# A group-norm kernel on one core: another engine leads the exit of the critical section, and most semaphores are cleared inside it

## The chip, the core and the metric

The kernel runs on one core of a Trainium2 chip. The core has five engines with their own instruction streams: PE (TensorE, matrix multiply), DVE (VectorE), ACT (ScalarE), POOL (GpSimd) and SP (SyncE), which here only issues DMA transfers and waits. The engines meet through numbered semaphores: an instruction can wait until a semaphore has reached a value, and can raise one when it is done. A DMA transfer raises its semaphore by 16 when it has landed.

The metric is the device time of the program in microseconds. Three runs of the kernel before gave 633.89, 633.71 and 632.71 us, median 633.71 us.

## The reference

The input x is bf16 of shape 128 x 1024 x 32 x 16 (134 MB), and so is the output. The 1024 channels fall into 32 groups of 32 channels; a group of one sample has 32 * 512 = 16384 numbers, which are brought to mean 0 and variance 1 and then scaled and shifted per channel:

```
xr = x.reshape(B, G, C // G, H, W)
mu = xr.mean(axis=(2, 3, 4), keepdims=True)
var = ((xr - mu) ** 2).mean(axis=(2, 3, 4), keepdims=True)
xn = (xr - mu) / jnp.sqrt(var + 1e-5)
xn = xn.reshape(B, C, H, W)
return xn * g[None, :, None, None] + b[None, :, None, None]
```

## The kernel before

One partition of the on-chip memory holds one group of one sample, so that a tile of 128 partitions holds 4 samples: 128 x 16384 bf16, 4 MB. There are 32 tiles and six slots for them (`xs`); a tile is loaded into its slot, normalised in place and stored from there, and the slot's next load waits until that store has landed.

Per tile, PE sums the partition's 16384 numbers with 32 matmuls against the identity into one PSUM tile (`sums`, L186 and L202). ACT takes a rough mean from the first channel (L210), then squares and sums the shifted numbers in four parts (L221), and takes the root of the variance (L230). DVE makes mean, variance, scale and bias from these (L237 to L277, instructions on a few numbers per partition) and applies them in 32 passes of 512 columns (L287). PE, ACT and DVE each run their part in a loop over rounds of six tiles; their waits name a semaphore per slot.

SP's stream is written out by hand, without a loop: L141 to L149. It issues six loads, and then alternately the store of a tile (L135, waits for DVE's last pass) and the load of a later one (L130, waits for an older store). All transfers go through SP's one queue. At the end, L150 and L151 let SP wait until the last store of each slot has landed. POOL only builds the identity at the start (L157, L167).

All of it stands in one critical section (L58), in which the framework orders nothing and adds no semaphore. What it adds lies around the section, and the change is about that. The instructions added carry the line L58 (entry and exit of the section) and L348 (the line of the launch that opens and closes the tile context; L337 is where the program object is made). They are:

- **Entry.** One engine, the section's leader, raises a semaphore, and all five wait for it in a branch. The leader is SP.
- **Exit.** The leader raises a second semaphore when it leaves the section (L58, semaphore 208 in the trace). Each of the five engines waits for it in a Drain (an instruction that lets the engine finish what it has begun) and then raises a semaphore of its own. The leader waits for those five in two event-semaphore instructions and a NOP.
- **End of the context** (L348). SP has one more Drain, which by the program waits for all engines; the waits are left out where SP has already made them. Then comes a barrier: every engine drains and raises the semaphore 96, POOL waits until the other four have, and lets them go by semaphore 97. POOL drains again and clears, in one instruction (EVENT_SEMAPHORE_RANGE_CLEAR), all semaphores that the context has given out, 99 to 212, which are 114. A second barrier of the same form ends the program.

Each semaphore of the kernel is made by a helper of two lines (L63), from the context, which is why the context clears them at its end:

```
def sem(name):
    return tc.alloc_semaphore(name)
```

Of the kernel before, what the change touches and what calls it, by code (L numbers as in the profile page):

```python
# [16 lines left out]
SLOTS = 6  # L17
# [5 lines left out]
def kernel(  # L23
# [13 lines left out]
    nc = tc.nc  # L37
# [17 lines left out]
    g_v = g.rearrange("(q k) -> q k", q=G)  # L55
    b_v = b.rearrange("(q k) -> q k", q=G)

    ctx.enter_context(tc.tile_critical())  # L58

    def sb(name, shape, dtype):  # L60
        return ctx.enter_context(nc.sbuf_tensor(name, shape, dtype))

    def sem(name):  # L63
        return tc.alloc_semaphore(name)

    xs = [sb(f"x{j}", [P, F], BF16) for j in range(SLOTS)]
    ps = [
# [32 lines left out]
    def sems(name):  # L100
        return [sem(f"{name}{j}") for j in range(SLOTS)]

    s_load = sems("load")
    s_store = sems("store")
    s_sum = sems("sum")
    s_shift = sems("shift")
    s_part = [sems(f"part{k}_") for k in range(SQ_PARTS)]
# [7 lines left out]
    s_bia = sems("bia")  # L115
    s_done = sems("done")
    s_gb = sem("gb")
    s_gbf = sem("gbf")
    s_eps = sem("eps")
    s_ones = sem("ones")  # L120
    s_half = sem("half")
    s_eye = sem("eye")

    sp, pe, act, dve, pool = nc.sync, nc.tensor, nc.scalar, nc.vector, nc.gpsimd

    def load(i):
        j, n = (i + FIRST) % SLOTS, i // SLOTS
        if n > 0:
            sp.wait_ge(s_store[j], 16 * n)
        sp.dma_start(out=xs[j][:], in_=x_v[i]).then_inc(s_load[j], 16)  # L130

    def store(i):
        j, n = (i + FIRST) % SLOTS, i // SLOTS
        sp.wait_ge(s_done[j], n + 1)
        sp.dma_start(out=o_v[i], in_=xs[j][:]).then_inc(s_store[j], 16)  # L135
# [10 lines left out]
    for i in range(NT):  # L146
        store(i)
        if i >= 1 and i + SLOTS - 1 < NT:
            load(i + SLOTS - 1)  # L149
    for j in range(SLOTS):  # L150
        sp.wait_ge(s_store[j], 16 * len(range((j - FIRST) % SLOTS, NT, SLOTS)))  # L151

# [169 lines left out]
            normalise(j, n)  # L322


# [1 line left out]
_INS = ['x', 'g', 'b']  # L326
_OUTS = [((128, 1024, 32, 16), 'bfloat16')]
# [25 lines left out]
```

## Time and profile before

| | |
|---|---|
| median of 3 runs | 633.71 us (632.71 to 633.89) |
| the profiled execution's own time | 633.21 us |
| its span, first to last instruction | 631.5 us |
| time outside the span (633.21 - 631.5) | 1.7 us |
| DMA, read and written | 268 MB, 425 GB/s over the span |
| ACT, DVE, PE busy | 519.3, 394.8, 284.3 us |
| last store issued on SP | 608.9 us |
| last store seen landed by SP (last L151) | 628.9 us |

The span is what lies between the first and the last instruction that carries a line of the program. Engine names with a q (SPq, POOLq) are the instructions that an engine's sequencer handles itself: waits, branches, drains, NOPs, clears, and DMA issues. In the view of one line's instructions, a row gives the engine, the operation and its count, the shortest, middle and longest duration in ns, and the start of the first and the last in us.

### The profile page before, as it was taken

Reading aid. Unit: us, or ns where it says so; the run is one execution under the profiler, and the core shown is the slowest. Engines: PE = TensorE matmul, PEld = TensorE weight load, DVE = VectorE, ACT = ScalarE, POOL = GpSimd, SP = SyncE. Lnnn points to the kernel's source line nnn. Section 1 sums busy time; section 2 is a strip of 40 time slices with the busy share of each in tenths; the row PEclk is TensorE's granted clock in tenths of the full one; section 3 lists DMA queues with packets and bytes.
Section 4 is the critical chain, followed back from the end, with each engine's and each line's share of the span. In section 5 each row is a group of like instructions: output and inputs, shape, how many; then the busy total and the mean of one; then the engine's idle time right before and its main releaser. Section 6 shows DMA issues by size and latency. Waiting matters only on the chain.

```text
span 631.5 us, 2991 instructions
## 1 busy us (share of the span) xinstructions
PE 284.3 (45%) x1024; PEld 3.3 (1%) x32; DVE 394.8 (63%) x1316; ACT 519.3 (82%) x354; POOL 0.8 (0%) x6
## 2 busy tenths in 40 slices
PE   1968405553445633456433654334553346543300
PEld 0000000000000000000000000000000000000000
DVE  0177777666666677777655676555775557765550
ACT  2999999999999999998788978889888888888800
POOL 0000000000000000000000000000000000000000
PEclk9999958765787667876678776778766787767755
DMA  8999999999999999999999999999999999999995
GB/s 363 430 430 413 440 438 432 431 430 430 432 432 428 432 430 432 432 432 432 430 432 438 434 432 432 436 440 436 430 432 434 432 432 432 434 432 432 432 432 233
DMA packets 9485, 268.51 MB, mean 425 GB/s; under 512 B 1288, under 2 KB 1288, under 8 KB 1288
## 3 DMA queue, kind: packets, MB, share of 16 engines
q1 hardware_dynamic: 9480, 268.46, 98.9%
q14 instruction: 4, 0.03, 0.0%
q8 instruction: 1, 0.02, 0.0%
HBM read 134.23 MB, written 134.22 MB: 425 GB/s over the span
## 4 chain that ended last, share of the span: by engine, by line
DMA 73%; ACT 18%; DVE 4%; issue 1%; SPq 1%; DVEq 0%; ACTq 0%
DMA out_dram<-x 66%; ACT js L221 17%; DMA x<-in_x_dram 7%; DVE x L287 3%; ACT ja L210 1%; SPq L130 1%; ACT std L230 0%; DVE jv L261 0%; DVE nd L252 0%; DVE d L248 0%; DVE bia L277 0%; DVE scl L273 0%; DVE rstd L271 0%; DVEq L247 0%; ACTq L307 0%
## 5 line engine op out<-in xcount | busy, mean ns | idle before, releaser
L221 ACT ACTIVATE js<-x,nshift 128x4096 bf16<-128x4096 bf16 x128 | 474.7, 3708 | 4.1
L287 DVE TENSOR_SCALAR x<-x,scl,bia 128x512 bf16<-128x512 bf16 x1024 | 333.6, 405 | 1.2
L186 PE MATMUL ps<-x,eye 128*128 128x512 bf16 x992 | 272.4, 443 | 0.0
L202 PE MATMUL ps<-x,eye 128*128 128x512 bf16 x32 | 18.4, 574 | 305.7 <-DMA x<-in_x_dram 305.7
L248 DVE TENSOR_TENSOR d<-negmean,nshift 128x1 f32<-128x1 f32 x32 | 5.1, 159 | 169.2 <-ACT js L221 169.2
L210 ACT ACTIVATE ja<-x 128x512 bf16<-128x512 bf16 x32 | 19.9, 623 | 47.5 <-DMA x<-in_x_dram 46.9
L230 ACT ACTIVATE std<-var,eps_t 128x1 f32<-128x1 f32 x32 | 9.4, 294 | 25.8 <-DVE jv L261 25.8
L237 DVE TENSOR_SCALAR_CACHE_REDUCE jd<-ps 128x512 bf16<-128x512 f32 x32 | 21.9, 685 | 13.4 <-PE ps L186 13.1
L221 ACT ACTIVATION_READ_ACCUMULATOR js<-x,nshift 128x1 f32 x128 | 23.9, 186 | 0.0
L271 DVE RECIPROCAL rstd<-std 128x1 f32<-128x1 f32 x32 | 5.2, 163 | 11.6 <-ACT std L230 11.6
L277 DVE SCALAR_TENSOR_TENSOR bia<-scl,negmean,bet 128x32 f32<-128x32 f32 x32 | 8.0, 251 | 1.1
L273 DVE TENSOR_SCALAR scl<-gam,rstd 128x32 f32<-128x32 f32 x32 | 7.7, 242 | 1.1
L179 DVE CAST gam<-gam_b 128x32 f32<-128x32 bf16 x1 | 0.2, 180 | 13.1 <-DMA bet_b<-in_b_dram 13.1
L261 DVE TENSOR_SCALAR_CACHE_REDUCE jv<-sq,nd 128x4 f32<-128x4 f32 x32 | 6.9, 217 | 1.1
L252 DVE TENSOR_SCALAR nd<-d 128x1 f32<-128x1 f32 x32 | 6.8, 214 | 1.1
L202 PEld LDWEIGHTS ps<-x,eye 128*128 128x128 bf16 x32 | 3.3, 103 | 577.3 <-DMA x<-in_x_dram 577.3
L210 ACT ACTIVATION_READ_ACCUMULATOR ja<-x 128x1 f32 x32 | 6.0, 186 | 0.0
L261 DVE DVE_READ_ACCUMULATOR jv<-sq,nd 128x1 f32 x32 | 2.6, 82 | 0.0
L237 DVE DVE_READ_ACCUMULATOR jd<-ps 128x1 f32 x32 | 2.6, 81 | 0.0
L177 ACT ACT_TABLE_LOAD x1 | 1.3, 1283 | 1.0 <-SPq L58 1.0
L154 DVE MEMSET eps_t<- 128x1 f32 x1 | 0.1, 59 | 1.1 <-SPq L58 1.1
L157 POOL TENSOR_SCALAR_AFFINE_SELECT half<-ones 128x128 bf16<-128x128 bf16 x1 | 0.3, 292 | 0.9 <-DVE ones L155 0.9
(8 smaller groups left out, 1.2 us busy)
## 6 DMA issues: line engine op xcount, KB each, us to landing
x<-in_x_dram SPq DMA_DIRECT2D x32, 4096.0 KB, 29.1
out_dram<-x SPq DMA_DIRECT2D x32, 4096.0 KB, 38.3
gam_b<-in_g_dram SPq DMA_DIRECT2D x1, 8.0 KB
bet_b<-in_b_dram SPq DMA_DIRECT2D x1, 8.0 KB
```

What stands on the lines that cost most here:

```text
L130: sp.dma_start(out=xs[j][:], in_=x_v[i]).then_inc(s_load[j], 16)
L186: return pe.add_instruction(mybir.InstMatmult(name=nc.get_next_instruction_name(), ins=[pe.lower_ap(rhs), first.ins[1]], outs=[first.outs[0]],
L202: m = pe.matmul(out=ps[j][:], lhsT=eye[:], rhs=xs[j][:, 0:MM_FREE], start=True, stop=False)
L210: act.activation(out=ja[:], in_=xs[j][:, 0:HW], func=ACT.Identity, scale=-1.0 / HW, accum_out=nshift[j][:],).then_inc(s_shift[j], 1)
L221: act.activation(out=js[:], in_=xs[j][:, k * SQ : (k + 1) * SQ], func=ACT.Square, bias=nshift[j][:], scale=1.0, accum_out=sq[j][:, k : k + 1],
L230: act.activation(out=std[j][:], in_=var[j][:], func=ACT.Sqrt, bias=eps_t[:], scale=1.0).then_inc(s_std[j], 1)
L237: dve.tensor_scalar(out=jd[:], in0=ps[j][:], scalar1=-inv_n, scalar2=None, op0=ALU.mult, op1=ALU.add, accum_out=negmean[j][:],).then_inc(s ...
L252: dve.tensor_scalar(out=nd2[j][:], in0=d[j][:], scalar1=d[j][:], scalar2=-1.0, op0=ALU.mult, op1=ALU.mult,).then_inc(s_nd2[j], 1)
L261: dve.tensor_scalar(out=jv[:], in0=sq[j][:], scalar1=inv_n, scalar2=nd2[j][:], op0=ALU.mult, op1=ALU.add, accum_out=var[j][:],).then_inc(s ...
L273: dve.tensor_scalar(out=scl[j][:], in0=gam[:], scalar1=rstd[j][:], scalar2=None, op0=ALU.mult).then_inc(s_scl[j], 1)
L277: dve.scalar_tensor_tensor(out=bia[j][:], in0=scl[j][:], scalar=negmean[j][:], in1=bet[:], op0=ALU.mult, op1=ALU.add,).then_inc(s_bia[j], 1)
L287: v = dve.tensor_scalar(out=xs[j][:, k * HW : (k + 1) * HW], in0=xs[j][:, k * HW : (k + 1) * HW], scalar1=scl[j][:, k : k + 1], scalar2=bi ...
```

## The change

The critical section gets two arguments: ACT is its leader (`sync_engine`), and POOL is not drained at its exit (`no_gpsimd_drain`). The kernel's semaphores, except the six of the stores and a new one named `gone`, are taken from the program object and not from the context, so that the context doesn't clear them. SP raises `gone` after it has issued the last store, and before its final waits. POOL waits for `gone` as the last thing in the section, and clears the kernel's own semaphores there as one range: 99 to 200, 102 of them. For the context's clear at the end, 13 are left: 201 to 213, which are the six of the stores, `gone`, and the six that the framework uses at entry and exit.

```
-    ctx.enter_context(tc.tile_critical())
+    ctx.enter_context(tc.tile_critical(
+            sync_engine=mybir.EngineType.Activation, no_gpsimd_drain=True
+        ))
...
+    all_sems = []
+
     def sem(name):
-        return tc.alloc_semaphore(name)
+        all_sems.append(nc.alloc_semaphore(name))
+        return all_sems[-1]
...
-    s_store = sems("store")
...
+    s_store = [tc.alloc_semaphore(f"store{j}") for j in range(SLOTS)]
+    s_gone = tc.alloc_semaphore("gone")
...
         if i >= 1 and i + SLOTS - 1 < NT:
             load(i + SLOTS - 1)
+    sp.sem_inc(s_gone, 1)
     for j in range(SLOTS):
         sp.wait_ge(s_store[j], 16 * len(range((j - FIRST) % SLOTS, NT, SLOTS)))
...
             normalise(j, n)
+    pool.wait_ge(s_gone, 1)
+    pool.sem_clear(range(all_sems[0].num, all_sems[-1].num + 1))
```

In the built program, this moves the following. At entry, ACT has the NOP that raises the semaphore, and SP no longer. At exit, ACT raises the leader's semaphore as soon as its own loop is done; the Drains of PE, DVE, SP and ACT and a NOP on POOL wait for it; ACT makes the three waits for the five engines. SP has no event-semaphore of the leader and no NOP; after the branch that ends its final waits comes its exit Drain, then two event-semaphore instructions and the Drain at the end of the context, which now carry the waits for the other engines, and then the barrier. The barriers, the second Drain of POOL and the order of clear and second barrier stay. The work inside the section is the same on every engine, instruction by instruction.

## The prediction

> **What bounds the kernel now.** I read the chain of waits first, then the waits on SP's own queue, then the DMA view, and last the rows of the added lines. The chain, by engine and line:
>
> ```profile
> DMA 73%; ACT 18%; DVE 4%; issue 1%; SPq 1%; DVEq 0%; ACTq 0%
> DMA out_dram<-x 66%; ACT js L221 17%; DMA x<-in_x_dram 7%; DVE x L287 3%; ACT ja L210 1%; SPq L130 1%; ACT std L230 0%; DVE jv L261 0%; DVE nd L252 0%; DVE d L248 0%; DVE bia L277 0%; DVE scl L273 0%; DVE rstd L271 0%; DVEq L247 0%; ACTq L307 0%
> ```
>
> The kernel is bound by its transfers: 268 MB through one queue at 432 GB/s in nearly every slice. The change touches none of them and no compute, so what it can move is what lies before the first load and after the last store. The waits of SP's queue show the end (who waits on whom; us in total, times, longest):
>
> ```profile
> SPq L151 <- DMA out_dram<-x: 19.6, 3, 9.7
> SPq L348 <- PEq L348: 1.3, 2, 1.1
> ```
>
> SP issues the last store at 608.9 us and then waits 19.6 us in L151. All other engines are idle there; that is the cover for anything that the change puts behind `gone`. The last store's semaphore is full at 628.895 us, the span ends at 631.493: the exit takes 2.598 us, and it is a pure chain. Its rows (answers for L58 and L348 from 628 us on):
>
> ```profile
> L58 SPq EVENT_SEMAPHORE  x3: 17/28/28, 629.1 to 629.4; - x3
> L58 POOLq DRAIN  x1: 41/41/41, 629.2 to 629.2; - x1
> L58 SPq DRAIN  x1: 13/13/13, 629.2 to 629.2; - x1
> L58 SPq NOP  x1: 17/17/17, 629.5 to 629.5; - x1
> ```
> ```profile
> L348 POOLq EVENT_SEMAPHORE  x4: 17/17/17, 630.1 to 631.4; - x4
> L348 POOLq DRAIN  x3: 34/34/216, 629.3 to 631.2; - x3
> L348 SPq DRAIN  x3: 7/7/123, 629.9 to 630.3; - x3
> L348 POOLq EVENT_SEMAPHORE_RANGE_CLEAR  x1: 656/656/656, 630.5 to 630.5; - x1
> ```
>
> To see: SP's exit waits lie between 629.1 and 629.5; its next Drain starts only at 629.9 and is the one of 123 ns; the clear of 114 semaphores takes 656 ns with every other engine waiting in the second barrier. The trace's start times of these instructions, in ns, are what I add up below.
>
> **The exit before, step by step** (start to start): landing to SP's wait 16 ns; to the branch 65; to SP's leader signal (629.135) 159; to SP's Drain 95; to the two event-semaphores 84 and 75; to the NOP 70 (629.459); to the Drain of L348 (629.919) 460; to the barrier's Drain 186 (630.105); to POOL's two barrier instructions 32 and 79; to POOL's Drain 81; to the clear 245 (that Drain took 216); to the Drain behind it 690; then 78, 78, 42 and, to the end, 63. Sum 2598.
>
> **Part 1, the clear.** 114 semaphores are cleared in 656 ns; in the trace the first goes down 21 ns after the start, the last 608 ns after the first, so 608/113 = 5.4 ns each and about 48 ns fixed. Thirteen cost 12 * 5.4 + 48 = 113 ns. Bounds: pure proportion, 656 * 13/114 = 75 ns, and three times the fixed part, 210 ns. I take 113: gain 543 ns, all on the path.
> The other 102 go to POOL in the section: about 590 ns after `gone`, from 609.3 to 609.9 us. Behind it on POOL stand only a NOP, a branch, a Drain and the barrier's wait; who waits for POOL is ACT (at exit) and SP (its end Drain), neither before 629.1. Cover 19 us; without it, it would cost 0.6 us.
> SP's `gone` signal stands behind the last store's issue and ahead of L151. Priced like L151's own 17 to 28 ns plus some 50 ns to the next, it ends near 609.3; SP's first L151 got through at 609.557, after 0.31 us of waiting. It costs nothing. The new queue order moves no transfer: all 66 are issued in the same order, ahead of it.
>
> At this place a rule differs. The Trainium skill, "Runtime: NRT & Kernel Launch", section "The ~15µs preamble/postamble breakdown", gives about 1.5 us for the runtime's own reset of 51 semaphores per engine, 29 ns each. By that the 101 fewer clears would be worth 3.0 us and the sum would be near 629.5 us. The trace's row for this instruction has a duration, so it decides.
>
> **Part 2, ACT leads the exit.** Before, the round from SP's signal over the Drains back to SP's NOP runs after the last landing. After, PE, DVE, POOL and ACT have signalled by about 610 us, and SP's Drain no longer waits for a signal either. SP's path becomes: wait 16, branch 65, exit Drain 159 (629.135), event-semaphores at 84 and 75, end Drain at 70 (629.364). One signal (95 ns) is gone, and the NOP's place goes to the Drain itself. ACT runs beside it: SP's exit Drain signals at 629.16, ACT's wait, NOP and barrier Drain follow at some 20, 72 and 65 ns (SP's rows again), 629.32, before SP. POOL's NOP for a Drain of 41 ns was beside the path and is beside it still: nothing.
> What follows depends on the 460 ns ahead of SP's Drain of L348. That Drain has no wait in the program; SP's three other Drains of the exit start 63 to 78 ns after the end of what stands ahead of them, and take 7 to 13 ns. So 390 ns of pause and 116 ns of length, 506 together, belong to something that the trace doesn't name. No packet of the instruction queue moves at that time; the only one near is at 630.56 us. Two readings:
> - It belongs to the place in SP's stream (the sixth instruction after the branch). After the change the sixth is the barrier's event-semaphore, where SP waits for POOL: POOL needs 32 + 79 + 81 + 245 + 113 + 34 + 78 = 662 ns from the start of SP's barrier Drain to its second gathering, and SP's 7 + 443 + 123 ns, one more Drain at 92 and its signal at some 25, 690 in all, fit in it but for 28 ns. Or it belongs to the NOP, which SP no longer has. Either way it goes: gain 506 ns.
> - It belongs to this Drain, or to leaving the section. Then it stays on the path: gain 0.
> I take the first, since SP's own Drains are the nearest rows, and none of the other three has it.
> The Trainium skill, "Perfetto Trace Analysis", section "Sequencer-only Instruction (DRAIN, etc)", says that the profiler's start is where the waits are satisfied, so that fetching and decoding lie ahead of it. By this a pause ahead of a Drain without waits is fetch and decode, a property of the place; the sum by it is the same -1.21 us, and no row here shows a fetch.
>
> What else goes on the path: 629.135 + 84 + 75 + 70 = 629.364 for the end Drain, +70 for the barrier's Drain 629.434; POOL +32, +79, +81, +245 = 629.871; clear and Drain +147; +78, +78, +42, +63 = 630.279. Against 631.493: **-1.21 us**, of which 0.54 the clear, 0.165 the round, 0.51 the pause. Without the pause: -0.71.
>
> **Part 3, ACT leads the entry.** SP raised the entry signal at 0.804 us and left its branch at 0.864; ACT, which came out of the start's barrier 5 ns after SP (0.726 against 0.721), left at 0.825. With ACT's NOP the signal comes near 0.81 and SP's branch at 0.83 to 0.88. Bounds for the first load: 0.03 us earlier, 0.05 later. I take 0. ACT's table load slips by some 70 ns; behind it stands a wait of 11.5 us for the first tile.
>
> **Sum.** The profiled execution took 633.21 us, 0.50 below the median of 633.71, inside the runs' 632.71 to 633.89. 633.21 - 1.21 = 632.00. The mean of the four times is 633.38; less 1.21 that is 632.17. I take **632.2 us**. About 0.2% (1.27 us) is what a measurement of this kernel can tell from no change, and my sum lies on that edge: -0.19% of its own execution, -0.24% against the median shown.
>
> **Rivals.**
> - *The pause stays* (second reading): 633.38 - 0.71 = 632.7 us. For it: it stands directly ahead of the only end Drain, which the change keeps. Against: POOL's Drains without a wait start after 64 to 67 ns.
> - *More goes than I count.* POOL's Drain ahead of the clear took 216 ns, its neighbours 34. If it is short after the change, with the clear already run once on POOL: 0.18 us more, and 0.03 from the entry: 633.38 - 1.42 = 632.0 us. Nothing in the trace says why it is long.
> - *Slower: the pause is what SP pays for a wait on other engines after leaving the section.* Then the two event-semaphores and the end Drain pay 0.51 us each where one instruction did: two more payments, 1.02, less the 0.71 of the other parts, so 0.31 us slower, 633.38 + 0.31 = 633.7 us. It turns slower than before with the second extra payment and passes 0.2% with the fourth (2.04 - 0.71 = 1.33; the barrier's Drain and event-semaphore of SP would have to pay too). Against: the same two event-semaphores ran at 84 and 75 ns in the trace before.
> - *The early clear does harm*: POOL's wait and clear would have to outlast the last stores, 19.6 us for work of 0.6. I give it nothing of its own.
>
> **How the numbers follow.** The pause goes: 0.55. It stays: 0.30. More goes: 0.09. Slower: 0.06. The runs scatter by 0.6 us to each side, so the bound of 0.2% cuts through the cases: 6 in 10 of the first, 3 in 10 of the second and 9 in 10 of the third end faster by over 0.2%: 0.33 + 0.09 + 0.08 = 0.50. Slower by over 0.2%: the last, with all its payments, 0.06. Within: 0.44. The range goes from the third case less 0.6 us (631.4) to the second plus 0.6 (633.3), which leaves out the slower case and the scatter's tails.
>
> **What would show it.** In the changed kernel: a clear of about 590 ns on POOL at 609.3 us and one near 113 ns at the end; from the last landing to the span's end 1.4 us instead of 2.6; SP's end Drain at about 0.45 us after the landing; first load at 1.0 us. It is wrong if the pause of 0.44 us stands ahead of SP's end Drain again (then 1.9 us), if the short clear takes over 0.2 us, if the first load starts over 0.1 us later, or if the transfers between first load and last landing take another time, which no edit explains.

## The result and the profile after

The changed kernel took 632.19 us (median of 12 runs, 631.15 to 633.46), the kernel before 633.76 us (12 runs, 632.71 to 635.34). The ratio is 0.9976, with a 95% interval of 0.9968 to 0.9984: 1.0 to 2.0 us faster. Here and below the ratio and its interval come from all runs together, so the ratio is not exactly the quotient of the two medians; the kernel before was run again beside each batch, which is why its median differs a little from place to place.

The profiled execution after took 633.28 us with a span of 631.6 us; the one before took 633.21 us with 631.5. The two spans don't show the gain: from the first load to the last landing the transfers took 627.88 us before and 629.25 us after, with the same instructions. Over the profiled executions of all kernels here, whose transfers are the same, this stretch goes from 627.2 us to 630.2 us. So I compare the exit alone, from the last landing (the last rise of a store's semaphore, 630.235 us after) to the span's end (631.568): 1.333 us, against 2.598 before. The time outside the span is 1.67 to 1.77 us in the 12 runs after and was 1.71 in the profiled one before.

The chain of waits after, by engine, is the chain before:

```profile
DMA 73%; ACT 18%; DVE 4%; issue 1%; SPq 1%; DVEq 0%; ACTq 0%
```

The waits of SP's own queue after (us in total, times, longest):

```profile
SPq L158 <- DMA out_dram<-x: 19.5, 3, 9.6
SPq L349 <- PEq L349: 0.7, 1, 0.7
SPq L360 <- SPq L360: 0.5, 1, 0.5
SPq L360 <- PEq L360: 0.2, 1, 0.2
```

SP still waits 19.5 us for the last stores behind its new signal. New is the row of 0.5 us in the barrier of L360, for which the profile names no engine but SP itself. There SP stands still for 458 ns, until 631.239 us, while ACT, DVE and PE leave the same wait for POOL at 630.93 to 630.94. Before, SP was the first of the four to leave it. That is the pause of 0.44 us from before, in another place.

The instructions of L334 (POOL's early clear), L156 (SP's new signal), and of L58 and L360 from 629 us on:

```profile
L334 POOLq EVENT_SEMAPHORE_RANGE_CLEAR  x1: 591/591/591, 610.7 to 610.7; - x1
```
```profile
L156 SPq EVENT_SEMAPHORE  x1: 17/17/17, 610.6 to 610.6; - x1
```
```profile
L58 SPq DRAIN  x1: 13/13/13, 630.5 to 630.5; - x1
L58 ACTq EVENT_SEMAPHORE  x1: 38/38/38, 630.5 to 630.5; - x1
L58 ACTq NOP  x1: 14/14/14, 630.6 to 630.6; - x1
```
```profile
L360 SPq EVENT_SEMAPHORE  x4: 17/22/28, 630.6 to 631.5; - x4
...
L360 SPq DRAIN  x3: 7/7/23, 630.7 to 631.3; - x3
...
L360 POOLq DRAIN  x2: 34/55/76, 631.0 to 631.2; - x2
L360 POOLq EVENT_SEMAPHORE_RANGE_CLEAR  x1: 109/109/109, 631.1 to 631.1; - x1
```

The clear at the end takes 109 ns instead of 656. SP's Drains of L360 begin at 630.7 us, 0.49 us after the landing (before, those of L348: 1.02), and the one of 123 ns is gone. POOL's Drain ahead of the clear takes 76 ns instead of 216. The early clear and SP's signal lie 19 us ahead of the end.

In start times, after the landing: the end Drain of SP at 485 ns (forecast 469), the barrier's Drain at 539 (539), POOL's first two barrier instructions at 572 and 650, its Drain at 731, the clear at 841, the second gathering (where POOL waits for the other four in the second barrier) at 1150, the end at 1333 (1384). SP's first load is issued at 0.985 us, 33 ns earlier than before.

### The profile page after: what moved, and what is told of

Same layout as the page of the kernel before. It is cut to its first block, busy times and chain, and to the rows that moved or that the text cites. A ratio compares the mean times of both kernels' runs of the same rounds, so it can differ in the third digit from the quotient of the medians.

```text
span 631.6 us, 2995 instructions
## 1 busy us (share of the span) xinstructions
PE 287.4 (46%) x1024; PEld 3.3 (1%) x32; DVE 394.9 (63%) x1316; ACT 519.4 (82%) x354; POOL 0.8 (0%) x6
## 4 chain that ended last, share of the span: by engine, by line
DMA 73%; ACT 18%; DVE 4%; issue 1%; SPq 1%; DVEq 0%; ACTq 0%
DMA out_dram<-x 67%; ACT js L228 17%; DMA x<-in_x_dram 7%; DVE x L294 3%; ACT ja L217 1%; SPq L136 1%; ACT std L237 0%; DVE jv L268 0%; DVE nd L259 0%; DVE d L255 0%; DVE bia L284 0%; DVE scl L280 0%; DVEq L58 0%; DVE rstd L278 0%; DVEq L254 0%
## 5 line engine op out<-in xcount | busy, mean ns | idle before, releaser
L193 PE MATMUL ps<-x,eye 128*128 128x512 bf16 x992 | 275.3, 447 | 0.0
L209 PE MATMUL ps<-x,eye 128*128 128x512 bf16 x32 | 18.6, 581 | 303.8 <-DMA x<-in_x_dram 303.8
```

The costliest lines, as they stand in the source:

```text
L193: return pe.add_instruction(mybir.InstMatmult(name=nc.get_next_instruction_name(), ins=[pe.lower_ap(rhs), first.ins[1]], outs=[first.outs[0]],
L209: m = pe.matmul(out=ps[j][:], lhsT=eye[:], rhs=xs[j][:, 0:MM_FREE], start=True, stop=False)
```

## The experiments

**Theories.** *Place*: the pause of 0.44 us ahead of SP's end Drain belongs to a place in SP's stream, a fixed number of instructions from its start; the change moved other instructions onto that place. *Drain*: it belongs to the end Drain, or to leaving the section with SP as leader. Both give the clear the same price, which the first run measures by itself. Where a kernel below was executed once only, its exit is given and its time proves nothing; times are compared for the four kernels with 12 runs.

**The early clear alone.** SP leads and POOL is drained, as before:

```
 (the changed kernel)
-    ctx.enter_context(tc.tile_critical(
-            sync_engine=mybir.EngineType.Activation, no_gpsimd_drain=True
-        ))
+    ctx.enter_context(tc.tile_critical())
```

> SP leads the section and POOL is drained as before; only the early clear of 102 semaphores and SP's signal for it are kept. Both theories: POOL's last clear 109 to 113 ns instead of 656, so 0.54 us off the path. Theory 'place' (the pause belongs to a fixed place in SP's stream): SP has one instruction more ahead of its final waits than the kernel before, so the pause of 0.44 us stands one instruction earlier after the branch, ahead of the NOP and no longer ahead of the Drain; exit from last landing to the span's end 2.60 - 0.54 = 2.05 us. Theory 'Drain' (it belongs to the end Drain): it stays ahead of that Drain; exit the same 2.05 us. Time about 0.55 us below the kernel before.

Measured: 633.06 us against 633.55, ratio 0.9988 (0.9975 to 1.0), so the time alone hardly shows it. Exit 1.842 us, 0.756 less than before. The exit rows of L58 and L358 from 629 us on:

```profile
L58 SPq EVENT_SEMAPHORE  x3: 17/28/28, 630.6 to 630.8; - x3
...
L58 SPq NOP  x1: 17/17/17, 631.3 to 631.3; - x1
```
```profile
L358 POOLq DRAIN  x3: 34/34/76, 630.7 to 631.9; - x3
L358 SPq DRAIN  x3: 7/7/48, 631.4 to 631.7; - x3
...
L358 POOLq EVENT_SEMAPHORE_RANGE_CLEAR  x1: 109/109/109, 631.8 to 631.8; - x1
```

The pause (438 ns) now stands between the event-semaphores at 630.8 us and the NOP at 631.3, one instruction earlier, as *place* says; the Drain follows after 58 ns. The exit is 0.2 us shorter than either theory had it: the clear gives 547 ns, POOL's Drain 140 that I hadn't counted, and SP's Drain is 48 ns long instead of 123: it ends 123 ns after the pause's end as before, but 75 of these have passed when it starts.

**The new leader alone**, with all semaphores cleared at the end:

```
 (the kernel before)
-    ctx.enter_context(tc.tile_critical())
+    ctx.enter_context(tc.tile_critical(
+            sync_engine=mybir.EngineType.Activation, no_gpsimd_drain=True
+        ))
```

> ACT leads and POOL is not drained at the section's exit; all 114 semaphores are cleared at the end, as before. The round over SP's signal and the NOP's place go: 0.165 us. Theory 'place': SP has one instruction less than the kernel before, the pause moves to the seventh after the branch, between the first barrier's event-semaphore and the second barrier's Drain, where SP waits for POOL's clear of 656 ns anyway; exit 2.60 - 0.165 - 0.51 = 1.92 us, or 1.78 if POOL's Drain of 216 ns is short here as well. Theory 'Drain': the pause stands ahead of SP's end Drain; exit 2.43 us. Time 0.7 to 0.8 us below the kernel before by the first, 0.2 by the second.

Measured: 632.49 us against 633.55, ratio 0.9987 (0.9975 to 1.0), so here too the exit decides. It is 1.925 us, which is *place* with POOL's Drain long (1.92). Its rows from 629 us on:

```profile
L350 SPq DRAIN  x3: 7/7/133, 630.8 to 631.5; - x3
...
L350 POOLq DRAIN  x2: 34/125/216, 631.0 to 632.0; - x2
...
L350 POOLq EVENT_SEMAPHORE_RANGE_CLEAR  x1: 656/656/656, 631.3 to 631.3; - x1
```

SP's long Drain is the last of its three, at 631.5 us, after a pause of 466 ns. POOL's clear of 656 ns began at 631.3, so SP paused while it waited for POOL anyway.

**Two instructions more ahead of it.** If the place decides, two idle signals on SP must put the pause back onto the path:

```
 (the changed kernel)
     sp.sem_inc(s_gone, 1)
+    for _ in range(2):
+        sp.sem_inc(s_gone, 1)
```

> The changed kernel with two more semaphore signals on SP behind the signal to POOL, where SP is idle for 0.2 us and then waits 19 us. Theory 'place': the pause stands two instructions earlier, ahead of SP's end Drain, and is on the path again: exit 1.33 + 0.46 - 0.09 = about 1.7 us. Theory 'NOP' or 'Drain' (it went with the old exit): the pause doesn't move, exit 1.33 us.

Measured: exit 1.758 us (one execution, 632.98 us). From 628 us on:

```profile
L362 SPq EVENT_SEMAPHORE  x4: 17/22/28, 629.8 to 631.2; - x4
...
L362 SPq DRAIN  x3: 7/7/123, 630.4 to 630.8; - x3
```

SP's first Drain here is the end Drain. It stands 439 ns after the event-semaphore ahead of it and takes 123 ns: the pause of the kernel before (443 and 123 ns), with ACT as the leader and without SP's NOP. *Drain* as "the old way of leaving" has fallen, and so has the NOP as the cause; the next run shows that the pause is no property of the end Drain either.

**Eight instructions more.** The same edit with `range(8)`, which moves the pause under the last stores:

> The changed kernel with eight more semaphore signals on SP behind the signal to POOL. Theory 'place': the pause lies ahead of the second of SP's final waits, under the last stores; SP's event-semaphore of the first barrier follows POOL's release at once, and the second barrier comes 0.09 us earlier: exit 1.24 us. Otherwise 1.33 us. Time against the changed kernel: nothing that can be measured; against the kernel before 1.3 us less.

Measured: exit 1.233 us, as *place* had it (1.24); 632.33 us against 633.55, ratio 0.9983 (0.9971 to 0.9995). From 628 us on:

```profile
L362 SPq DRAIN  x3: 7/7/7, 629.6 to 629.9; - x3
...
L362 POOLq EVENT_SEMAPHORE_RANGE_CLEAR  x1: 109/109/109, 630.0 to 630.0; - x1
```

All three Drains of SP at L362 take 7 ns. No pause is left behind the landing: the longest gap in SP's stream that isn't a wait for POOL is the 124 ns behind its branch. This has the shortest exit of all, 0.10 us less than the changed kernel; in time the two can't be told apart.

**The same in the kernel before.** Eight idle signals on an unused semaphore, nothing else:

```
 (the kernel before)
+    for _ in range(8):
+        sp.sem_inc(s_pad, 1)
     for j in range(SLOTS):
         sp.wait_ge(s_store[j], 16 * len(range((j - FIRST) % SLOTS, NT, SLOTS)))
```

> The kernel before, with eight semaphore signals on SP behind the last store and one more semaphore to clear; neither leader nor clear is changed. Theory 'place': the pause moves under the last stores; the exit loses 0.39 us of pause and perhaps 0.12 of the long Drain, 2.60 us becomes 2.09 to 2.21; about 0.4 to 0.5 us faster, which five rounds can just about tell. Theory 'it belongs to the exit': 2.60 us.

Measured: exit 2.080 us, 0.52 less than before and just under what *place* had (2.09 to 2.21); 633.19 us against 633.61, ratio 0.9993 (0.9983 to 1.0002), so the time alone doesn't show it. From 629 us on:

```profile
L351 POOLq DRAIN  x3: 34/34/222, 630.3 to 631.7; - x3
L351 SPq DRAIN  x3: 7/7/7, 630.5 to 630.8; - x3
...
L351 POOLq EVENT_SEMAPHORE_RANGE_CLEAR  x1: 658/658/658, 631.0 to 631.0; - x1
```

0.52 us of the exit before was the pause and the long Drain behind it, and eight instructions that do nothing take them off the path. The two kernels with eight idle signals have no pause in the exit, so between them the leader's round can be read by itself: from the landing to SP's barrier Drain it is 683 ns here and 532 ns in the changed kernel with eight more, 0.15 us less.

**POOL's Drain at the section's exit.** The changed kernel without `no_gpsimd_drain`:

> The changed kernel, but POOL drained at the section's exit again. POOL's Drain of about 41 ns lies at 611 us, 19 us ahead of the end: exit 1.33 us as in the changed kernel. If the missing Drain is what made POOL's Drain ahead of the last clear short (76 instead of 216 ns), that one is 216 again and the exit 1.43 us, the pause hiding part of it.

Measured: exit 1.333 us, POOL's Drain ahead of the last clear 76 ns. The argument `no_gpsimd_drain` is worth nothing here.

**Why POOL's Drain ahead of the clear got short.** First I put an early clear of one unused semaphore on POOL into the kernel before, and as a control a semaphore signal in its place:

```
 (the kernel before; the control has pool.sem_inc(s_pad, 1))
+    pool.sem_clear(s_pad)
     act.wait_ge(s_eps, 1)
```

> The kernel before, with a clear of one unused semaphore on POOL near the start and so 115 to clear at the end. If POOL's Drain ahead of its clear is long (216 ns) because that clear is POOL's first, it is 76 ns here: exit 2.60 - 0.14 + 0.005 = 2.46 us, the clear 661 ns. If it has to do with the length of the clear or with the exit's order, it stays 216 and the exit 2.60 us.

> The control to the run with the early clear: a semaphore signal in its place on POOL, one instruction more in POOL's stream but no clear. If an earlier clear is what shortens the Drain: 216 ns, exit 2.60 us. If it is only the place in POOL's stream: 76 ns, exit 2.46 us.

Measured: 223 ns in both, exits 2.605 and 2.607 us. That a clear, of one semaphore, had already run isn't the reason. What is left is an early clear of many, or the number cleared at the end. So I cleared the 102 twice, by taking them from the context again and keeping POOL's clear in the section:

```
 (the changed kernel)
-        all_sems.append(nc.alloc_semaphore(name))
+        all_sems.append(tc.alloc_semaphore(name))
```

> The changed kernel, but the 102 semaphores are cleared in the section and once more with the rest at the end: 115 there. If the length of POOL's Drain goes with the number that is cleared behind it, it is 216 to 223 ns; if an earlier large clear shortens it, 76. The clear 660 ns by 5.4 ns each. SP's pause lies ahead of the first barrier's event-semaphore as in the changed kernel and is hidden. Exit 1.33 - 0.09 + 0.55 = 1.79 us with the short Drain, 1.93 with the long one.

and left 73 for the end, with 42 cleared early:

```
 (the changed kernel)
     def sem(name):
+        if len(all_sems) == 42:
+            return tc.alloc_semaphore(name)
```

> The changed kernel with 42 semaphores cleared in the section and 73 left for the end. Clear at the end 109 + 60 * 5.4 = 434 ns, the one in the section 266. POOL's Drain ahead of it, if its length goes with the number in proportion, 76 + 60 * 1.4 = 160 ns; otherwise 76 or 220. Exit 1.33 - 0.09 + 0.325 = 1.57 us with the short Drain, 1.65 with the middle one, 1.71 with the long one.

Measured: exits 1.934 and 1.646 us, as the case "by number" had them (1.93 and 1.65). The early clear of 42 took 266 ns, as forecast. The rows of the clear that is done twice, then of the one in parts:

```profile
L360 POOLq DRAIN  x2: 34/128/223, 628.9 to 629.9; - x2
L360 POOLq EVENT_SEMAPHORE_RANGE_CLEAR  x1: 657/657/657, 629.2 to 629.2; - x1
```
```profile
L362 POOLq DRAIN  x2: 34/96/157, 629.9 to 630.5; - x2
L362 POOLq EVENT_SEMAPHORE_RANGE_CLEAR  x1: 434/434/434, 630.1 to 630.1; - x1
```

POOL's Drain ahead of the clear takes 76, 157 and 216 ns for 13, 73 and 114 semaphores, about 1.4 ns more for each; the clear itself 109, 434 and 656, 5.4 ns more for each. The clear done twice has the changed kernel's instructions in the same order, and only the range at the end differs (115 against 13): its Drain takes 223 ns against 76, so the range sets it and no early clear does. Why a Drain that stands ahead of a clear takes longer with the clear's size isn't shown by these runs.

## Why the prediction was right, and where it was off

The mechanism was right in its main terms: the clear, the round and the pause went off the path, and the exit became 1.27 us shorter where 1.21 were forecast. That the time hits the forecast to 0.01 us (632.19 against 632.2) is luck. The sum started from 633.38 us, the mean of four executions, and 12 runs give the kernel before 633.76; it took off 1.21 us, and the medians differ by 1.57. The two errors, 0.38 and 0.36 us, cancel. By its steps:

- **The clear.** 113 ns forecast, 109 measured, at the end; 590 forecast and 591 measured in the section. The gain of 0.54 us is right, but it isn't all that the early clear brings: the term "to the clear 245 (that Drain took 216)" was carried over unchanged, and the Drain takes 76. That is 0.14 us more, close to the size that the rival "more goes than I count" gave it (0.18), but that rival's condition, that the clear had already run once, was wrong; the number of semaphores sets it.
- **SP's signal.** It starts 46 ns behind the last store's issue and takes 17 ns; SP's next wait still had to wait 0.25 us. It costs nothing, as said.
- **The round.** End Drain forecast at 469 ns after the landing, measured 485; the barrier's Drain 539 and 539. The round itself was forecast at 0.165 us; the two kernels with eight idle signals give 0.15.
- **The pause.** The first reading is right in its first form. The pause moved with the count of SP's instructions in every run: ahead of the sixth instruction after the branch in the kernel before and after (the new signal takes the place of the entry's NOP in SP's stream), of the fifth with one more ahead, of the seventh with one less, of the fourth with two more, and out of the exit with eight more. Counted over the whole trace it is always the same place: in all ten kernels whose exit shows a pause it stands ahead of SP's 80th recorded instruction, whether that is a Drain, a NOP or an event-semaphore. It hides behind POOL less well than forecast: SP left it 0.30 us after the other engines had left the same wait, and POOL's second gathering stood 93 ns longer for SP. The prediction had found 28 ns there and put them at nothing in its sum. POOL was faster by the 140 ns of its Drain and 4 of the clear, and SP by 79 (611 ns from its barrier Drain to the gathering, 690 forecast).
- **The entry.** The first load is 33 ns earlier, the better bound.
- **The sum.** 2598 - 1333 = 1265 ns in the exit, forecast 1214: clear 547, Drain 140, and 671 for round and pause (the barrier's Drain stands 1210 ns after the landing before and 539 after), less the 93. The 140 and the 93 were not in the sum, and they cancel in part. With the 33 of the entry that is 1.30 us. The measured gain between medians is 1.57 us, and its interval of 1.0 to 2.0 holds 1.30; the other 0.27 us isn't explained by anything in the traces, and need not be. The same sum, against the median shown, had been said to be -0.24%; the ratio is 0.9976.
- **The signs.** The signs of the mechanism came true: the clears, the end Drain, an exit of 1.33 us for 1.4, the first load. One sign of being wrong came too: the transfers between first load and last landing took another time, 1.37 us more in the profiled execution after. As the same stretch goes over 3 us between the kernels here with the same transfers in it, the sign can't tell the change from scatter, and it should not have been one.

The two parts alone shorten the exit by 0.756 and 0.673 us, 1.43 together, while both at once give 1.265. The 0.16 us between these are the 93 ns of the pause that the short clear no longer covers, and some 70 ns that the early clear alone gained when the pause moved ahead of the NOP. With the early clear, POOL is done sooner, and less of the pause is covered: with 73 or 115 semaphores left for the end the 93 ns are gone, and the exits are 1.646 and 1.934 us as forecast on that ground.

The slower rival (a pause for each wait on other engines) fell: SP's two event-semaphores stand 94 and 80 ns apart from what is ahead of them, and no exit has more than one pause.

On the rules weighed: the 29 ns per semaphore, an estimate from the Trainium skill's 1.5 us for 51 ("Runtime: NRT & Kernel Launch", "The ~15µs preamble/postamble breakdown"), belong to the runtime's own reset. The range clear measured 5.4 ns each, 6.8 with the Drain ahead of it, so the sum by the row was the right one. (By the 29 ns the prediction's sum comes to 632.2 + 0.54 - 2.97 = 629.8 us, not the 629.5 that it gave.) The rule of "Perfetto Trace Analysis", "Sequencer-only Instruction (DRAIN, etc)", that fetch and decode lie ahead of the reported start, agrees with a pause that follows the place in the stream; no row shows a fetch.

## What to carry to other kernels

When transfers bound a kernel and can't be touched, the exit after the last landing is still a chain that can be added up instruction by instruction, and whatever need not wait for the landing can go under it: here a clear worth 0.69 us, and a round of signals worth 0.15. A pause ahead of one bookkeeping instruction should be tested by shifting the stream before it is put down to that instruction; here eight idle instructions under a wait of 19 us were worth 0.5 us by themselves. Where the change is smaller than the scatter of the transfers (3 us between the profiled executions here), compare the stretch that the change touches, not the spans.

## What the hardware showed that I had not expected

A pause of 0.44 to 0.47 us stands at one place of SP's stream in all ten kernels whose exit shows it, and instructions that do nothing move it onto other work. A Drain that follows it ends about 0.12 us after the pause's end (123, 133 and 123 ns long where it stands directly behind; 48 and 23 ns where another instruction lies between). A packet of the queue that the profile calls instruction (8192 bytes) follows. In the kernel before the pause ended at 629.919 us and the packet started at 630.558; in the changed kernel the two times are 631.239 and 631.871 (the span had ended at 631.568, so the exit doesn't wait for the packet), and with two more instructions 630.383 and 631.017. The DMA view from 629 us on has one such packet in the kernel before and one after, in this order:

```profile
q14 instruction: 1, 0.01, 1.1%
```
```profile
q14 instruction: 1, 0.01, 0.8%
```

With eight more there is none behind the landing; the last one starts at 613.6 us, under the last stores. That the packet moves with SP's pause goes well with the refill of instruction memory in blocks that the Trainium skill describes ("Runtime: NRT & Kernel Launch", "Instruction fetch mechanics"), the crossing of which it calls mostly hidden. The page's blocks are of 16 KiB and the packet here has 8192 bytes; and the pause here was on the path with 0.52 us. That the pause is the sequencer's part of that refill is the likely reading; no run here shows what SP does in it.

The range clear costs 5.4 ns per semaphore (109 ns for 13, 656 for 114), and the Drain ahead of it 1.4 ns per semaphore of the range that follows (76 and 216 ns).
